# Two weight pieces moved behind the second group's output, and VectorE's order in the first slots

## The chip, the cores and the metric

The kernel runs on one core of one Trainium2 chip. The metric is device microseconds of one execution. A core has five engines with an instruction stream of their own: TensorE (PE in the profile, its weight loads PEld), VectorE (DVE), ScalarE (ACT), GpSimd (POOL) and SyncE (SP), which issues nearly all DMAs here. Each engine runs its instructions in the order in which the program wrote them and waits on semaphores for the others.

## The reference, cut to what matters

Sparse attention of 4 batches, 8 heads, 576 positions and head size 64 (half of the heads look at the last 32 positions, the other half at every fourth of the last 128) gives a matrix of 2304 tokens by 512. Two feed-forward layers of width 2048 follow, each `(act(x @ w_in)) @ w_out`:

```
scores = scale * q @ k.T; scores = where(mask, scores, -1e9)
attn = exp(scores - max(scores)); attn = attn / (sum(attn) + 1e-9); x = attn @ v
h = x @ moe_w_in;  g = maximum(h, 0) + alpha * minimum(h, 0);  x = g @ moe_w_out
h = x @ moe2_w_in; g = where(h >= 1, h, where(h <= -1, 0, (h + 1)**2 / 4)); y = g @ moe2_w_out
```

## The kernel before, in words

All is float32 in accuracy. TensorE gets there by three products of two halves: a matrix is split into a high half (a ScalarE cast, L327) and a low half (the rest, a subtraction on GpSimd or VectorE, L328), and a product is low x high + high x low + high x high (L513 to L515 for the first layer's input side, L706 to L708 for its output side).

Attention is cut into 24 groups of three blocks, six for each batch. The first six groups (batch 0) run at the very start, in the loop `for i in range(NGB)`; the others are spread over the feed-forward slots that follow. Group i of the first six goes through: scores on TensorE (`e_scores`), maximum and subtraction on VectorE and the exponential on ScalarE (`e_exp`, L190, L191, L193), transposes (`a_turn`, L212, copied by ScalarE in L214), values (`e_values`, 48 small matmuls in L205) with the division on VectorE (`a_norm`, L229 to L231), and transposes back (`a_out`, L238) with a ScalarE copy to X (L256). The loop is a pipeline written out by hand: turn i holds the scores of group i, the transposes of i - 1, the exponential of i, the output of i - 2 and the values of i - 1, in this order on every engine.

Weights come in 512 KB pieces, 128 x 1024 words of 32 bits, of which `w_load` (L272) loads one into a staging buffer (five of them at the start). VectorE makes a piece's 128 x 512 float32 from it in three operations that `w_make` returns: L321, L322 and L315. `conv(k)` runs the next k of these operations of the list of pieces. The first two write their intermediate into the weight's own buffer in SBUF as long as `w0_tile` holds nothing, and into a PSUM bank after that. When a piece of the input weights is done, the next `w_cut()` splits it into halves (ScalarE L327, GpSimd L328); the pieces at the start are (rows 0, 1, 2 of w_in), w_out 0, w_in 3, and so on.

In the loop the pieces 0 and 1 are loaded among the six groups' own inputs (the set `FIRST` in L757) and converted at the end of turns 0 and 2 (L817). At the end of turn 3 the first 512 tokens' chunk 0 is split (`x_split`, low half on GpSimd), GpSimd clears a buffer (L821), and SyncE then loads group 6 and more pieces; turn 4 splits chunk 1. Behind the loop come the first layer's rows 0 and 1, one chunk of the input after the other (`f_h(n0, 0, (0,))`, `f_h(n0, 1, (0,))`, ...), with the last two groups' remaining steps between them, three more `conv` calls, and one small VectorE operation that turns alpha into 1 - alpha (L847). Then come the slots: one feed-forward row each, with the activation (ScalarE L650, VectorE L653), the conversions (`EARLY`: five in the first slot) and one point at which attention moves on.

Of the kernel before, what the change touches and what calls it, by code (L numbers as in the profile page):

```python
# [10 lines left out]
F32 = mybir.dt.float32  # L11
# [5 lines left out]
ALU = mybir.AluOpType  # L17
# [3 lines left out]
DM, DFF = 512, 2048  # L21
NT = B * S
P = 128
# [31 lines left out]
NX = 9  # L55
NR = 4

FIRST = (0, 2)

EARLY = (5, 6)  # L60
READY = 12
# [26 lines left out]
def attention_then_two_ffns(ctx: ExitStack, tc: tile.TileContext, a0, aqk, av, w1i, w1o, w2i, w2o, alpha, masks, ident, out, out_l):  # L88
    nc = tc.nc
# [10 lines left out]
    ps_a = ctx.enter_context(tc.tile_pool(name="ps_a", bufs=1, space=bass.MemoryType.PSUM))  # L100
# [3 lines left out]
    al = const.tile([P, NF], F32, name="al")  # L104
# [9 lines left out]
    sc_t, s_t, pT_t, o_t = {}, {}, {}, {}  # L114
# [81 lines left out]
    def e_values(i):  # L196
        pT = pT_t.pop(i)
        ps = ps_e.tile([P, 2, TW], F32, tag="o2", name="o_ps")
        v = e_in[i][:, QK:].rearrange("p (n j d) -> p n j d", n=GS, j=4)
        for n in range(GS):  # L200
            for j in range(4):
                r = slice(j * SUB, (j + 1) * SUB)
                for h in range(2):
                    p = slice(h * D, (h + 1) * D)
                    nc.tensor.matmul(ps[r, h, n * DS:(n + 1) * DS], pT[p, n, r], v[p, n, j], start=True, stop=True)  # L205
        a_norm(i, ps[:, :, :GS * DS].rearrange("p h (n d) -> p n h d", n=GS))
# [19 lines left out]
    def a_norm(i, ps):  # L226
        o = tmp(i).tile([P, GS, 2, D], F32, tag="o", name="o")
        rs = st_p.tile([P, GS, 2, 1], F32, tag="rs", name="rs")
        nc.vector.tensor_scalar(rs, ps[:, :, :, D:], 1e-9, None, ALU.add)  # L229
        nc.vector.reciprocal(rs, rs)  # L230
        nc.vector.tensor_tensor(o, ps[:, :, :, :D], rs.to_broadcast([P, GS, 2, D]), ALU.mult)  # L231
        o_t[i] = o
# [32 lines left out]

    st_free = [f"v{i}" for i in range(NX - NST, NX)]

    def w_load(ph, f, part):
        w = ((w1i, w1o), (w2i, w2o))[ph][part]
        tag = st_free.pop(0)  # L270
        st = xv_p.tile([P, DM, 2], I32, tag=tag, name="st") if tag in xv_tags else pools[tag].tile([P, DM, 2], I32, tag=tag, name="st")
        nc.sync.dma_start(st.rearrange("p a b -> p (a b)"), w[f].bitcast(I32))  # L272
        cv[ph, f, part] = (st, tag)

# [2 lines left out]
    w0_tile = [None]  # L277
# [48 lines left out]
    def two(hi, lo, src, low_on):  # L326
        nc.scalar.activation(hi, src, AF.Copy)  # L327
        low_on.tensor_tensor(lo, src, hi.bitcast(F32), ALU.subtract)  # L328
# [29 lines left out]
    def w_split(n, f):  # L358
        t = r_slot((n, f))
        two(t[:, 0], t[:, 1], wi[n[0], f], nc.vector if n == PAIRS[0] and f < 2 else nc.gpsimd)  # L360
        wt[n, f] = t
        b = base.get((n[0], f // 2))
        if b:
            b[1] -= 1
            if not b[1]:
                x_free.append(b[0])

    def w_cut():
        while cut:
            w_split(*cut.pop(0))  # L370
# [46 lines left out]
    def x_slot(n):  # L417
        tag = x_free.pop(0)
        x_tags.setdefault(n, []).append(tag)
        return pools[tag].tile([P, 2, TW], F32R, tag=tag, name="xv")  # L420

    def x_split(n, c, on_pool=False):
        ph, t = n
        t0, w = TILES[ph][t]
        at = 0
        if w < TW and c % 2:
            x, at = xt[n, c - 1][0], w
        else:
            x = x_slot(n)
        two(x[:, 0, at:at + w], x[:, 1, at:at + w], X[c][:, t0:t0 + w], nc.gpsimd if on_pool else nc.vector)  # L430
        xt[n, c] = (x, at)
# [298 lines left out]
    with tc.manual_schedule(), ExitStack() as late:  # L730
# [19 lines left out]
        pend_l = pieces(0)  # L750
        pend_w = list(pend_l)

        for i in range(NGB):
            a_load_qk(i)
            a_load_v(i)
            if i in FIRST:
                w_load(*pend_l.pop(0))  # L757
            if i == 1:
                nc.sync.dma_start(mask[:, 2 * GS:], masks[:, 2 * GS:])
        nc.sync.dma_start(al, alpha)  # L760
# [26 lines left out]
        def conv(k):  # L787

            for _ in range(k):
                if not todo and pend_w and pend_w[0] in cv:  # L790
                    todo.extend(w_make(*pend_w.pop(0)))
                if todo:
                    todo.pop(0)()
                    if not todo:
                        more()
# [8 lines left out]
        for i in range(NGB):  # L804
            e_scores(i)
            if i >= 1:
                a_turn(i - 1, ps_a, "a")
            e_exp(i)
            if i >= 2:
                a_out(i - 2, ps_a, "w")  # L810
            else:
                fill(2)
            if i >= 1:
                e_values(i - 1)
            w_cut()
            if i in FIRST:
                conv(3)  # L817
            if i == 3:
                x_split(n0, 0, True)

                nc.gpsimd.memset(qk[0], 0.0)  # L821
                hold = False
                a_load_qk(NGB)
                w_load(*pend_l.pop(0))
                w_load(*pend_l.pop(0))
                a_load_v(NGB)
                more()
            if i == 4:
                x_split(n0, 1, True)
        w_cut()  # L830
        f_h(n0, 0, (0,))
        f_h(n0, 1, (0,))
# [10 lines left out]
        f_h(n0, 1, (2,))  # L843
        x_split(n0, 3)
        w_cut()
        conv(1)
        nc.vector.tensor_scalar(al, al, -1.0, 1.0, ALU.mult, ALU.add)  # L847
        a_load_qk(NGB + 1)
        a_load_v(NGB + 1)
        f_h(n0, 0, (3,))  # L850
        f_h(n0, 1, (3,))
        first.close()
        w0_tile[0] = lambda: ps_a.tile([P, DM], F32, tag="w", name="w_ps")
        pools_q = [f"{g}{i}" for g in ("qk", "vz") for i in range(2)]
        pools.update({g: wq for g in pools_q})
        wl_p = late.enter_context(tc.tile_pool(name="wl_p", bufs=1))
# [53 lines left out]
        def one_y():  # L910
            f_y(*pend_y.pop(0))
# [4 lines left out]
        def slot(n, f, k):  # L916
            nn = after_n[n]
            if k not in (1, 2):
                split_pending()
            if k > 1 and (n, f) not in wt:  # L920
                w_cut()
            if n == LAST and f == NF - 1:
                wo_split((n, 0), f)
            if k > 1 or n == LAST:
                f_h(n, f)
            early = f < 2 and k > 1
            if early:
                one_y()
            if n == PLAIN[0] and f == NF - 3:
                pend_l.extend(pend_2)  # L930
            if n == PLAIN[0] and f == NF - 1:
                pend_w.extend(pend_2)
            if n in PLAIN[:2] and f >= NF - NC:
                x_split(nn, f - NF + NC, n == PLAIN[1])
            if k in (0, 1):
                ops = EARLY[k]
            elif n == n0:
                ops = 6
            elif n != LAST:
                ops = 1 if n == PLAIN[1] else 3  # L940
            else:
                ops = 0
            attention_point()
            if k == 2:
                split_pending()
            b0, b1 = BEFORE[n[0]]
            b0 = min(ops, b0) if k else 0
            g = f_g(n, f, lambda: conv(b0))
            ops -= b0
            first_ops = min(ops, b1 if k else 3)  # L950
            w_cut()
            conv(first_ops)
            f_cut(n, f, g)
            if k == 0:
                wo_split((n, 0), f)
            ahead = 2 if n == PLAIN[0] else 3
            for i in range(1, ahead + 1):
                if f + i < NF:
                    ready(n, f + i)
                elif nn and nn not in PAIRS:  # L960
                    ready(nn, f + i - NF)
            if n == PLAIN[2]:
                if f == 9:
                    turn = iter(range(1 << 30))
                    x_work.extend(x_seven(nn, lambda: ps_a.tile([P, TW], F32, tag="w" if nxt < NG or at else "wa"[next(turn) % 2], name="room")))
                if NF - 4 <= f < NF - 1:
                    p_weights(nn, 0, f - NF + 4)
                if READY <= f < NF - 1:
                    wo_split((n, 0), f)
                if f >= READY:  # L970
                    more_x((6, 6, 3, len(x_work))[f - READY])
                if f == NF - 1:
                    p_weights(nn, 0, 3)
                if f == NF - 1:
                    r_free.extend(x_free[:2])
                    del x_free[:2]
            if n == LAST and f % 2 == 0 and 4 <= f // 2 + 3 < NF // 2:
                w_base(1, f // 2 + 3)
            if k >= 2 and not early:
                one_y()  # L980
            pend_y.append(((n, 0), f))
            attention_point()
            if n == PLAIN[2] and f in (9, 10):
                more_x(3)
            conv(ops - first_ops)
            more()

        k = 0
# [235 lines left out]
```

## Time and profile before

| | |
|---|---|
| median of 3 runs | 848.47 us (847.82 to 849.39) |
| the profiled execution's own time | 848.41 us |
| its span, first to last instruction | 846.3 us |
| TensorE busy, matmuls | 831.4 us, 98% |
| VectorE busy | 514.4 us, 61% |
| ScalarE busy | 459.3 us, 54% |
| GpSimd busy | 483.1 us, 57% |
| mean granted TensorE clock | 0.996 of 2.4 GHz |

Times in the profile's rows are microseconds from the span's start; a mean of one instruction is in ns. A busy time is the union of an engine's instructions. The profiled execution took 2.1 us more than its span, for what lies before the first and behind the last instruction.

### The profile page before, as it was taken

Reading aid. Unit: us, or ns where it says so; the run is one execution under the profiler, and the core shown is the slowest. Engines: PE = TensorE matmul, PEld = TensorE weight load, DVE = VectorE, ACT = ScalarE, POOL = GpSimd, SP = SyncE. Lnnn points to the kernel's source line nnn. Section 1 sums busy time; section 2 is a strip of 40 time slices with the busy share of each in tenths; the row PEclk is TensorE's granted clock in tenths of the full one; section 3 lists DMA queues with packets and bytes.
Section 4 is the critical chain, followed back from the end, with each engine's and each line's share of the span. In section 5 each row is a group of like instructions: output and inputs, shape, how many; then the busy total and the mean of one; then the engine's idle time right before and its main releaser. Section 6 shows DMA issues by size and latency. Waiting matters only on the chain.

```text
span 846.3 us, 14045 instructions
## 1 busy us (share of the span) xinstructions
PE 831.4 (98%) x5232; PEld 681.3 (81%) x5234; DVE 514.4 (61%) x831; ACT 459.3 (54%) x883; POOL 483.1 (57%) x411
## 2 busy tenths in 40 slices
PE   6999999999999999999999999999999999999998
PEld 3667778998777878888888888888888888888897
DVE  4798787666775676776688565665326556530132
ACT  3444444665435465555444677675437666553375
POOL 2465656777434677767448676754662332346485
PEclk9899999999999999999999999999999999999999
DMA  8788665864640025444287735343835553538120
GB/s 303 240 252 228 203 171 179 257 196 135 191 129 26 1 75 180 144 154 169 100 312 301 282 142 204 127 173 121 327 125 203 196 198 125 174 134 313 69 82 25
DMA packets 54978, 147.43 MB, mean 174 GB/s; under 512 B 5632, under 2 KB 13440, under 8 KB 54912
## 3 DMA queue, kind: packets, MB, share of 16 engines
q1 hardware_dynamic: 54624, 146.39, 50.9%
q8 instruction: 41, 0.67, 0.3%
q14 instruction: 25, 0.20, 0.1%
q10 hardware_dynamic: 288, 0.16, 0.1%
HBM read 101.97 MB, written 44.56 MB: 173 GB/s over the span
## 4 chain that ended last, share of the span: by engine, by line
PE 92%; DVE 4%; ACT 1%; issue 1%; DMA 1%; ACTq 0%; DVEq 0%
PE y L706 14%; PE y L707 14%; PE y L708 14%; PE h_ps L544 9%; PE h_ps L546 9%; PE h_ps L545 9%; PE h_ps L513 5%; PE h_ps L515 5%; PE h_ps L514 5%; PE o_ps L223 2%; PE s_ps L149 1%; PE t_ps L212 1%; PE y L691 1%; PE y L692 1%; PE y L693 1%
## 5 line engine op out<-in xcount | busy, mean ns | idle before, releaser
L328 POOL TENSOR_TENSOR wol<-wo,woh 128x512 fp32r<-128x512 f32 x153 | 201.8, 1326 | 74.5 <-ACT woh L327 64.4
L328 POOL TENSOR_TENSOR wr<-wb,wr 128x512 fp32r<-128x512 f32 x60 | 77.8, 1297 | 130.3 <-ACT wr L327 130.3
L706 PE MATMUL y<-gh,wol 128*128 128x512 f32 (+1 forms) x384 | 146.3, 381 | 0.0
L708 PE MATMUL y<-gl,woh 128*128 128x512 f32 (+1 forms) x384 | 142.8, 372 | 0.0
L707 PE MATMUL y<-gh,woh 128*128 128x512 f32 (+1 forms) x384 | 142.8, 372 | 0.0
L328 POOL TENSOR_TENSOR wr<-wi,wr 128x512 fp32r<-128x512 f32 x50 | 64.6, 1293 | 121.2 <-ACT wr L327 119.9
L544 PE MATMUL h_ps<-xv,wr 128*128 128x512 f32 x336 | 131.3, 391 | 0.5 <-DVE gl L666 0.4
L546 PE MATMUL h_ps<-xv,wr 128*128 128x512 f32 x336 | 130.8, 389 | 0.0
L545 PE MATMUL h_ps<-xv,wr 128*128 128x512 f32 x336 | 130.8, 389 | 0.0
L327 ACT ACTIVATE woh<-wo 128x512 fp32r<-128x512 f32 x153 | 93.5, 626 | 65.7 <-PE y L708 51.3
L513 PE MATMUL h_ps<-xv,wr 128*128 128x512 f32 (+1 forms) x256 | 89.9, 351 | 0.2
L514 PE MATMUL h_ps<-xv,wr 128*128 128x512 f32 (+1 forms) x256 | 86.3, 337 | 0.2 <-DVE xv L328 0.2
L515 PE MATMUL h_ps<-xv,wr 128*128 128x512 f32 (+1 forms) x256 | 86.4, 337 | 0.0
L706 PEld LDWEIGHTS y<-gh,wol 128*128 128x128 f32 x384 | 72.2, 188 | 15.2 <-issue 2.0
L708 PEld LDWEIGHTS y<-gl,woh 128*128 128x128 f32 x384 | 72.2, 188 | 13.0 <-DVE gl L581 0.4
L707 PEld LDWEIGHTS y<-gh,woh 128*128 128x128 f32 x384 | 72.3, 188 | 11.8
L544 PEld LDWEIGHTS h_ps<-xv,wr 128*128 128x128 f32 x336 | 63.1, 188 | 15.8 <-issue 1.4
L706 PE MATMUL y<-gx,wol 128*128 128x512 f32 x192 | 74.8, 390 | 0.0
L707 PE MATMUL y<-gx,woh 128*128 128x512 f32 x192 | 74.7, 389 | 0.0
L708 PE MATMUL y<-gx,woh 128*128 128x512 f32 x192 | 74.7, 389 | 0.0
L566 DVE SCALAR_TENSOR_TENSOR h_ps<-h_ps,g 128x512 f32<-128x512 f32 x64 | 44.6, 697 | 48.3 <-ACT g L558 48.3
L546 PEld LDWEIGHTS h_ps<-xv,wr 128*128 128x128 f32 x336 | 63.1, 188 | 13.2
(130 smaller groups left out, 1552.3 us busy)
## 6 DMA issues: line engine op xcount, KB each, us to landing
gd<-XA SPq DMA_DIRECT2D x42, 512.0 KB, 3.3
gx<-gd SPq DMA_DIRECT2D x42, 512.0 KB, 6.5
wb<-whole SPq DMA_DIRECT2D x30, 512.0 KB, 5.1
st<-w1i SPq DMA_DIRECT2D x16, 512.0 KB, 5.2
st<-w1o SPq DMA_DIRECT2D x16, 512.0 KB, 5.3
st<-w2i SPq DMA_DIRECT2D x16, 512.0 KB, 4.2
st<-w2o SPq DMA_DIRECT2D x16, 512.0 KB, 4.9
kept<-wr SPq DMA_DIRECT2D x16, 512.0 KB, 2.7
```

The lines of the kernel that those rows point to most:

```text
L327: nc.scalar.activation(hi, src, AF.Copy)
L328: low_on.tensor_tensor(lo, src, hi.bitcast(F32), ALU.subtract)
L513: nc.tensor.matmul(ps[:, :w], r[:, 1, cs], x[:, 0, xs], start=(c == 0), stop=False)
L514: nc.tensor.matmul(ps[:, :w], r[:, 0, cs], x[:, 1, xs], start=False, stop=False)
L515: nc.tensor.matmul(ps[:, :w], r[:, 0, cs], x[:, 0, xs], start=False, stop=(c == NC - 1))
L544: nc.tensor.matmul(o, w[:, 1, cs], x[:, 0], start=start and m == 0, stop=False, skip_group_check=not start)
L545: nc.tensor.matmul(o, w[:, 0, cs], x[:, 1], start=False, stop=False, skip_group_check=not start)
L546: nc.tensor.matmul(o, w[:, 0, cs], x[:, 0], start=False, stop=m == 1, skip_group_check=not start)
L566: ve.scalar_tensor_tensor(ps, ps, 1.0, t, ALU.max, ALU.min)
L706: nc.tensor.matmul(o, wl[:, cs], gh[:, :w], start=(i == 0), stop=False)
L707: nc.tensor.matmul(o, wh[:, cs], gh[:, :w], start=False, stop=False)
L708: nc.tensor.matmul(o, wh[:, cs], gl[:, :w], start=False, stop=(i == NF - 1))
```

## The change

`FIRST` becomes (3, 4): the first two pieces are converted at the end of turns 3 and 4. They are no longer loaded among the groups' inputs; in turn 2, behind the second group's `a_norm`, VectorE copies one element of that group's output into each staging buffer, and the two loads wait for those copies. The 1 - alpha operation moves to the end of turn 4. The PSUM intermediate of the conversions begins one `conv` earlier, with the fourth piece. In the first slot two conversions instead of three run ahead of the point at which attention moves on, and three instead of two behind it.

```
-FIRST = (0, 2)
+FIRST = (3, 4)
...
-    def w_load(ph, f, part):
+    def w_load(ph, f, part, behind=None):
...
+        if behind is not None:
+            nc.vector.tensor_copy(st[:, 0, :1].bitcast(F32), behind[:, 0, 0, :1])
         nc.sync.dma_start(st.rearrange("p a b -> p (a b)"), w[f].bitcast(I32))
...
             a_load_v(i)
-            if i in FIRST:
-                w_load(*pend_l.pop(0))
...
                 e_values(i - 1)
+            if i == 2:
+                for _ in FIRST:
+                    w_load(*pend_l.pop(0), o_t[1])
             w_cut()
             if i in FIRST:
                 conv(3)
...
             if i == 4:
                 x_split(n0, 1, True)
+                nc.vector.tensor_scalar(al, al, -1.0, 1.0, ALU.mult, ALU.add)
...
         w_cut()
+        w0_tile[0] = lambda: ps_a.tile([P, DM], F32, tag="w", name="w_ps")
         conv(1)
-        nc.vector.tensor_scalar(al, al, -1.0, 1.0, ALU.mult, ALU.add)
...
         first.close()
-        w0_tile[0] = lambda: ps_a.tile([P, DM], F32, tag="w", name="w_ps")
...
-            first_ops = min(ops, b1 if k else 3)
+            first_ops = min(ops, b1 if k else 2)
```

## Rows read from the trace of the kernel before

**Rows 1.** The page: busy us, share, instructions; the instruction queue's packets, MB, share.
```profile
PE 831.4 (98%) x5232; PEld 681.3 (81%) x5234; DVE 514.4 (61%) x831; ACT 459.3 (54%) x883; POOL 483.1 (57%) x411
...
q8 instruction: 41, 0.67, 0.3%
```
**Rows 2.** Stretches: length, busy by PE, PEld, DVE, ACT, POOL; clock, DMA, GB/s.
```profile
36.30:44.70 8.40, 7.84 (x58) 5.51 (x56) 8.11 (x14) 3.99 (x8) 3.30 (x3) 1.00 1.06 281
44.70:56.00 11.30, 9.95 (x88) 7.51 (x88) 10.92 (x20) 4.64 (x10) 7.60 (x6) 1.00 0.93 291
56.00:80.00 24.00, 23.86 (x195) 18.13 (x194) 20.11 (x35) 11.25 (x22) 15.30 (x12) 1.00 0.74 210
```
**Rows 3.** TensorE's instructions in order: start, length, line, operands, count, idle before and releaser.
```profile
14.47 0.72 PE L205 MATMUL o_ps<-e_in,pT 64*32 64x65 f32 x48 [1.63 <-ACT s L193]
...
17.23 0.42 PE L205 MATMUL o_ps<-e_in,pT 64*32 64x65 f32 x23 [0.32 <-ACT pT L214]
20.74 0.66 PE L205 MATMUL o_ps<-e_in,pT 64*32 64x65 f32 x25 [3.08 <-issue]
...
24.14 0.98 PE L205 MATMUL o_ps<-e_in,pT 64*32 64x65 f32 x48
...
29.11 0.39 PE L513 MATMUL h_ps<-xv,wr 128*128 128x512 f32 x1
```
**Rows 4.** DMA in 17.66:18.2, 18.2:18.3; GB/s by 40 slices in 17.66:20.74, 20.74:24.
```profile
q1 hardware_dynamic: 105, 0.18, 92.7%
...
q8 instruction: 1, 0.02, 69.1%
...
GB/s 327 365 489 250 408 290 185 330 62 43 41 43 50 0 41 0 41 41 0 41 0 81 41 0 41 41 41 3 4 0 3 4 0 0 0 0 0 0 0 0
...
GB/s 0 0 0 0 0 0 0 0 0 0 0 0 201 0 0 0 0 0 0 0 0 0 0 0 0 0 0 0 0 0 0 0 0 0 0 0 0 0 0 0
```
**Rows 5.** Stretches of 2 us, columns as in rows 2 (the clock is third from the end).
```profile
12.00:14.00 2.00, 0.84 (x8) 0.70 (x7) 1.11 (x2) 1.22 (x4) 1.27 (x1) 1.00 1.02 391
...
20.00:22.00 2.00, 1.26 (x47) 0.79 (x55) 0.47 (x3) 1.31 (x4) 1.12 (x1) 0.50 0.03 8
...
26.00:28.00 2.00, 1.75 (x74) 1.34 (x57) 1.26 (x3) 0.75 (x2) 1.28 (x1) 0.82 0.84 226
```
**Rows 6.** DMA issues at 0.74 and 1.66 us: KB, us from issue to landing.
```profile
e_in<-a SPq DMA_DIRECT2D x1, 416.0 KB, 3.7
...
st<-w1i SPq DMA_DIRECT2D x1, 512.0 KB, 5.3
```
**Rows 7.** VectorE's instructions in order.
```profile
15.22 0.17 DVE L229 TENSOR_SCALAR rs<-o_ps 128x6 f32<-128x6 f32 x1 [1.93 <-PE o_ps L205]
...
16.12 0.42 DVE L321 TENSOR_SCALAR wi<-st 128x512 int32<-128x512 int32 x1
...
17.91 0.55 DVE L190 TENSOR_REDUCE mx<-s_ps 128x6 f32<-128x384 f32 x1
...
35.37 1.52 DVE L321 TENSOR_SCALAR wo<-st 128x512 int32<-128x512 int32 x1
36.81 0.16 DVE L847 TENSOR_SCALAR al<-al 128x16 f32<-128x16 f32 x1
37.09 0.75 DVE L653 SCALAR_TENSOR_TENSOR g<-g,al,h_ps 128x512 f32<-128x512 f32 x1
```
**Rows 8.** ScalarE's instructions in order.
```profile
19.15 0.52 ACT L193 ACTIVATE s<-s 128x384 f32<-128x384 f32 x1 [1.97 <-DVE s L191]
...
36.28 0.60 ACT L650 ACTIVATE g<-h_ps 128x512 f32<-128x512 f32 x1 [1.03 <-PE h_ps L515]
```
**Rows 9.** GpSimd's instructions in order.
```profile
20.88 1.27 POOL L328 TENSOR_TENSOR wr<-wi,wr 128x512 fp32r<-128x512 f32 x1 [7.42 <-ACT wr L327]
...
23.32 1.17 POOL L821 MEMSET qk<- 128x1280 f32 x1
```
**Rows 10.** VectorE by line in 36.3:56: count, busy us, mean ns, idle before.
```profile
L321 DVE TENSOR_SCALAR w_ps<-st 128x512 int32<-128x512 int32 x6 | 4.2, 692 | 0.1
```

More of the change, by code (lines that the diff above doesn't have):

```diff
@@ L56 @@
 NR = 4
-FIRST = (0, 2)
+FIRST = (3, 4)
 EARLY = (5, 6)
@@ L266, in attention_then_two_ffns, with w_load @@
     st_free = [f"v{i}" for i in range(NX - NST, NX)]
-    def w_load(ph, f, part):
+    def w_load(ph, f, part, behind=None):
         w = ((w1i, w1o), (w2i, w2o))[ph][part]
@@ L271, in w_load @@
         st = xv_p.tile([P, DM, 2], I32, tag=tag, name="st") if tag in xv_tags else pools[tag].tile([P, DM, 2], I32, tag=tag, name="st")
+        if behind is not None:
+            nc.vector.tensor_copy(st[:, 0, :1].bitcast(F32), behind[:, 0, 0, :1])
         nc.sync.dma_start(st.rearrange("p a b -> p (a b)"), w[f].bitcast(I32))
@@ L755, in attention_then_two_ffns @@
             a_load_v(i)
-            if i in FIRST:
-                w_load(*pend_l.pop(0))
             if i == 1:
@@ L814, in attention_then_two_ffns @@
                 e_values(i - 1)
+            if i == 2:
+                for _ in FIRST:
+                    w_load(*pend_l.pop(0), o_t[1])
             w_cut()
@@ L829, in attention_then_two_ffns @@
                 x_split(n0, 1, True)
+                nc.vector.tensor_scalar(al, al, -1.0, 1.0, ALU.mult, ALU.add)
         w_cut()
@@ L845, in attention_then_two_ffns @@
         w_cut()
+        w0_tile[0] = lambda: ps_a.tile([P, DM], F32, tag="w", name="w_ps")
         conv(1)
-        nc.vector.tensor_scalar(al, al, -1.0, 1.0, ALU.mult, ALU.add)
         a_load_qk(NGB + 1)
@@ L852, in attention_then_two_ffns @@
         first.close()
-        w0_tile[0] = lambda: ps_a.tile([P, DM], F32, tag="w", name="w_ps")
         pools_q = [f"{g}{i}" for g in ("qk", "vz") for i in range(2)]
@@ L949, in slot @@
             ops -= b0
-            first_ops = min(ops, b1 if k else 3)
+            first_ops = min(ops, b1 if k else 2)
             w_cut()
```

## The prediction

> **What bounds the kernel now.** I read the page's busy shares first. TensorE is busy 831.4 of 846.3 us and no other engine passes 61% [rows 1], so only a stretch in which TensorE is not full can change the time. The stretches come next: from 56 to 80 us TensorE is busy 23.86 of 24 us, and from 36.3 to 56 it lacks 1.9 us while VectorE is busy 19.0 of 19.7 [rows 2]; before that it waits for whatever ends a short chain. Both edits lie before 43 us. After that each microsecond by which the start ends earlier or later reaches the end one for one, so the whole question is when the start ends.
>
> The instruction order of that start is the third view. TensorE stands still twice: 1.63 us up to 14.47 and 3.08 us up to 20.74, the second in the middle of 48 like matmuls (23 before it, 25 after) [rows 3]. The page's instruction queue has 41 packets of 16 KB (0.67 MB / 41); TensorE has 10,466 instructions, 255 for each packet [rows 1]. Between the two stops lie 127 matmuls with as many weight loads (48 + 50 + 3 + 3 + 23), 254. So both are stops for instructions. The packet that ends the second one is not among the transfers up to 18.2 us and is there at 18.2 to 18.3, when the queue of loads runs dry [rows 4]; TensorE goes on about 2.5 us later. After that stop the granted clock is 0.5, which is the 1.2 GHz level; it is 2.4 GHz after the shorter stop and again from 26.7 us (0.82 of 26 to 28 at two levels) [rows 5].
>
> By the Trainium skill (Runtime: NRT & Kernel Launch, section Instruction fetch mechanics) instructions come in 16 KiB blocks by a DMA queue of the engine, and the cost of a block's end is mostly hidden. The packet size agrees with the trace; hidden it is not here, with 3.08 us.
>
> **Part 1, the two weight pieces.** Removed from the front of the load queue: 2 x 512 KB of about 6 MB. The queue moves about 0.4 MB per us there [rows 5], so it runs dry 2.6 us earlier, at 15.6 instead of 18.2. The second stop shrinks, but not by all of that: a block's end is crossed at 14.47, and the packet for the block after that cannot come at once: behind the crossing at 20.74, with no load queued, it came in the 13th of 40 slices of 20.74 to 24, about 1.0 us later [rows 4]. Before, some of the 16 engines had loads until 19.8 (the bytes in the 40 slices of 17.66 to 20.74 end in the 28th), so until 17.2 now. With the packet at 15.6 to 17.2 TensorE goes on at 18.1 to 19.7; bounds 17.66 (no stop) and 20.74 (as before). I take 19.4, nearer the late end, because the packet has to pass the loads of its own engine.
>
> What is late next? Three things move onto VectorE behind it. Each conversion of a piece is L321, L322, L315: 16.12 to 17.91, 1.79 us; the three operations of a group's output are 0.90 (15.22 to 16.12); maximum and subtraction are 1.24 (17.91 to 19.15) [rows 7, 8]. Before, the pieces were converted right behind the scores of group 0 and the output of group 1, and TensorE's stops hid the delay. Now they stand in groups 3 and 4, where scores, maximum, subtraction, output and conversion are one chain. Step by step:
> - Group 1's output ends at 16.12 as before. Two copies of one element: nearest are the 0.17 for 6 elements and nothing; 0.3 for both with their gaps. SyncE then issues the two loads at 16.4; nothing is queued behind them but the loads of group 6, which wait for a GpSimd memset until about 22.
> - The pieces land: a first load of 416 KB on an empty queue took 3.7 us, one of 512 KB behind others 5.3 [rows 6]. So the first lands at 20.1 to 21.7; I take 20.4, as the queue is almost empty, and the second 1.3 us (512 KB) later.
> - Group 2's output starts on VectorE at 20.0 (19.4, the last 25 matmuls 0.5, a gap) and ends at 20.9. Conversion 1.79, maximum and subtraction 1.24, group 3's output 0.90, conversion 1.79, the 1 - alpha operation 0.18 (0.16 [rows 7] and a gap), maximum and subtraction 1.24. Sum 7.14: group 5's subtraction ends at 28.0.
> - Then the second piece is one cast away from TensorE. ScalarE first does group 5's exponential and group 3's output copy, then the high half, and GpSimd the low half: before, from exponential to GpSimd's end, 19.15 to 22.15, 3.0 us [rows 8, 9]. That chain was done at 22.15 and hidden; now it ends at 31.0, and TensorE's first matmul of feed-forward row 1, which ran at 29.11, waits for it [rows 3]. In TensorE's queue behind it stand group 5's transposes, its values, and all that follows to the first slot. Cost: 1.9 us.
> - One collision on top. L321 takes 0.42 us when GpSimd is idle; at 35.37 it took 1.52, with a GpSimd cast of the same time beside it [rows 7]. The first piece's L321 now falls at 20.9, beside the cast of the first token chunk (1.27) and the memset of 128x1280 (1.17), which move forward to 19.7 to 22.1 [rows 9]. Bounds 0 and 1.1 for it. The nearest row is the one at 35.37, so I take 1.1. The second piece's L321 comes ahead of GpSimd's next cast; 0. Part 1 is +3.0 us.
>
> By the Trainium skill (SBUF — State Buffer, Who interferes with whom) the pair of ports that VectorE and GpSimd share is an exclusive lock, and a VectorE operation with two SBUF inputs also stands still for a GpSimd operation that reads SBUF. The 1.52 us agree with the first half. By the second half L322 or L315 of the second piece, whose intermediate still lies in SBUF, would wait for a cast of 1.27 too; no row of before shows it, and the sum would be 1.3 us higher.
>
> **Part 2, VectorE's order.** The fourth piece's L321 at 35.37 writes to PSUM now: 0.69, as the six later ones that do so, instead of 1.52, and the alpha operation is gone from the place. That frees 1.0 us of VectorE, but the operation after them (37.09) needs ScalarE's result, which was ready at 36.88 (36.28 + 0.60) [rows 7, 8, 10]. So only 0.14 us comes forward (37.09 to 36.95); the rest becomes a wait. Taking the maximum ahead of one conversion lets TensorE transpose group 6 sooner, but VectorE has the same work to do up to 56 us and bounds that stretch [rows 2], so I cost it at nothing. Part 2 is -0.14 us, between 0 and -1.0.
>
> **Sum.** +3.0 - 0.14 = +2.9 on the profiled execution's 848.41 us: 851.3. The median shown is 848.47, 0.06 higher, which is nothing here.
>
> **The rivals.**
> - *A wash.* No collision, and the instruction packet comes at 15.6: then TensorE goes on at 18.1, the landing at 20.1 to 20.4 sets the first conversion instead of group 2's output, and the same sum costs 1.1 to 1.4 us; with 0.14 to 1.0 from part 2 that is +0.1 to +1.3: 849.2. For it: the memset may simply wait for VectorE. Against: it needs both.
> - *The clock falls again.* In my forecast TensorE stands from 29.7 (row 0's matmuls done) to 32.1, and 2 us before that for group 5's scores. A stop of 1.63 us left the clock at 2.4 GHz, one of 3.08 did not [rows 3, 5]; mine lie between. At half clock 48 small matmuls took 0.98 against 0.72 [rows 3], a third more; a matmul of 512 columns should lose more, up to double. The clock came back 6 us after the work did. On some 5.4 of the 6.3 us from 29.11 to 35.37 (the rest is other engines' work) that is 1.8 to 3.9; with 2.9, 854.2.
> - *The second stop stays*, because something else than the loads makes it: TensorE goes on at 20.74, 1.3 us later than I say: 852.6. Against it: the packet came as the queue of loads ran dry [rows 4]. The rule of the Trainium skill above (Runtime: NRT & Kernel Launch, Instruction fetch mechanics), with a fetch that is hidden, would make this the case.
> - *Not slower.* Both stops go, as loads of weights no longer stand between those of groups 1 and 3. TensorE then starts group 1's values at 13.1, the pieces are issued at 15.1 and land at 18.8 (3.7 later), and the chain from there (7.14 with 3.0 behind it) ends at 28.9, 0.2 before 29.11; if the freed 1.0 us of part 2 also counts in full, 847.2. The place that decides is the landing of the first piece: each microsecond before 18.8 is one more. Against: the queue of loads moves 0.39 MB per us at the first stop [rows 5] and will be as full there as it was.
>
> **How the numbers follow.** Forecast 0.38 (850.2 to 852.6), clock 0.21, stop stays 0.05, wash 0.21, not slower 0.15, of which 0.09 lies beyond 0.2%. 0.2% is 1.7 us, about what a measurement of this kernel can tell from nothing. So slower 0.64, the same 0.27 (0.21 + 0.06), faster 0.09. The range leaves out the far end of the clock case and most of the gains: 847.4 to 855.5; the slower cases alone span 850.2 to 855.5.
>
> **What would show it.** Right: the second stop about 1.3 us long; the two pieces issued at 16.4 and landed by 20.4 and 21.7; L321 of the first piece over 1 us; TensorE waiting at L513 of row 1 for GpSimd's cast, at 31 to 32; L321 of the fourth piece at 0.69 with a wait for ScalarE behind it. Wrong: row 1's first matmul before 29.1, or the operation of 37.09 earlier than 36.9 in the profile after. The clock line tells the third case apart. If the time from 56 us on is not the same in both profiles, the premise of the first paragraph falls.

## The result, and the profile after

| | before | changed |
|---|---|---|
| median | 848.50 us (4 runs, 847.82 to 849.39) | 855.19 us (4 runs, 854.47 to 856.57) |
| ratio | | 1.0078, 95% interval 1.0064 to 1.0092 |
| the profiled execution's time, span | 848.41, 846.3 | 855.31, 853.3 |

Slower by 0.78%, inside the range and on its far side: 3.9 us more than the 851.3 forecast. The change adds two lines above the ones it shifts, so L321, L322, L315 of before are L323, L324, L317 here, L513 is L515, L653 is L655 and L328 is L330.

TensorE's instructions in the changed kernel (columns as in [rows 3], whose rows these answer to):
```profile
14.84 0.72 PE L205 MATMUL o_ps<-e_in,pT 64*32 64x65 f32 x48 [1.93 <-ACT XA L256]
...
17.61 0.43 PE L205 MATMUL o_ps<-e_in,pT 64*32 64x65 f32 x23 [0.32 <-ACT pT L214]
18.37 0.43 PE L205 MATMUL o_ps<-e_in,pT 64*32 64x65 f32 x25 [0.33 <-issue]
...
23.04 0.30 PE L205 MATMUL o_ps<-e_in,pT 64*32 64x65 f32 x3 [1.55 <-issue]
25.11 0.50 PE L173 MATMUL s_ps<-mask,idt 128*128 128x192 bf16 x2 [1.77 <-DVE s L191]
...
33.82 0.74 PE L515 MATMUL h_ps<-xv,wr 128*128 128x512 f32 x1 [3.34 <-POOL wr L330]
```
The second stop is 0.33 us instead of 3.08, so at 18.37 TensorE is 2.4 us ahead of before. At 25.11 it is level, and at row 1's first matmul it is 4.7 us behind, waiting for GpSimd's cast of the second piece. That is the forecast's place, and 1.7 us later than its 32.1. What stands between is VectorE's chain, to be read against [rows 7]:
```profile
15.60 0.16 DVE L229 TENSOR_SCALAR rs<-o_ps 128x6 f32<-128x6 f32 x1 [2.23 <-PE o_ps L205]
...
16.62 0.21 DVE L273 COPY st<-o 128x1 f32<-128x1 f32 x2
...
20.41 2.06 DVE L323 TENSOR_SCALAR wi<-st 128x512 int32<-128x512 int32 x1 [0.53 <-DMA st<-w1i]
...
25.86 0.42 DVE L323 TENSOR_SCALAR wi<-st 128x512 int32<-128x512 int32 x1
...
27.04 1.65 DVE L317 SCALAR_TENSOR_TENSOR wi<-st,wi 128x512 int32<-128x512 int32 x1
28.61 1.24 DVE L833 TENSOR_SCALAR al<-al 128x16 f32<-128x16 f32 x1
...
30.41 0.56 DVE L191 TENSOR_TENSOR s<-s_ps,mx 128x384 f32<-128x384 f32 x1
```
Three operations are far over what they take alone: 2.06 (0.42 alone), 1.65 (0.69) and 1.24 (0.16). GpSimd in the same time ([rows 9]):
```profile
19.81 1.28 POOL L330 TENSOR_TENSOR xv<-XA,xv 128x512 fp32r<-128x512 f32 x1 [14.97 <-ACT xv L329]
21.02 1.17 POOL L824 MEMSET qk<- 128x1280 f32 x1
26.86 1.28 POOL L330 TENSOR_TENSOR wr<-wi,wr 128x512 fp32r<-128x512 f32 x1 [4.67 <-ACT wr L329]
28.10 1.72 POOL L330 TENSOR_TENSOR xv<-XA,xv 128x512 fp32r<-128x512 f32 x1
32.50 1.26 POOL L330 TENSOR_TENSOR wr<-wi,wr 128x512 fp32r<-128x512 f32 x1 [2.69 <-ACT wr L329]
```
L323 runs from 20.41 to 22.47: through the rest of the cast (to 21.09) and the whole memset (to 22.19), and then the 0.3 us it needs. L317 ends 0.55 us behind the cast of 26.86, the 1 - alpha operation just behind the cast of 28.10, which itself took 1.72 instead of 1.28, with L317 ahead of it (in e5_clear below, where L317 takes 0.69, the same cast takes 1.29).

Stretches of the changed kernel (columns as in [rows 5]):
```profile
24.00:30.00 6.00, 4.89 (x107) 3.56 (x107) 5.76 (x10) 2.70 (x5) 2.96 (x2) 0.50 0.97 291
30.00:34.00 4.00, 0.66 (x3) 0.18 (x2) 2.02 (x6) 1.42 (x3) 1.26 (x1) 0.93 1.04 336
34.00:38.00 4.00, 4.00 (x59) 3.11 (x60) 0.34 (x2) 1.57 (x4) 0.00 (x0) 0.58 0.21 80
```
VectorE is the full engine from 24 to 30; TensorE does 0.66 us of work from 30 to 34; the clock is at 1.2 GHz twice, in 24 to 30 and again in most of 34 to 38, behind the stops of 1.55 and 1.77 and the stop of 3.34 us.

Part 2's place, to be read against the last lines of [rows 7] (the fourth piece's L323, then the first slot's activation):
```profile
41.28 0.69 DVE L323 TENSOR_SCALAR w_ps<-st 128x512 int32<-128x512 int32 x1
42.83 0.75 DVE L655 SCALAR_TENSOR_TENSOR g<-g,al,h_ps 128x512 f32<-128x512 f32 x1 [0.86 <-ACT g L652]
```
0.69 us, and a wait of 0.86 us for ScalarE behind it, as forecast. Here the kernel is 5.74 us behind before (42.83 to 37.09).

### The profile page after: what moved, and what is told of

Its sections match the earlier page's. It is cut to its first block, busy times and chain, and to the rows that moved or that the text cites. A ratio compares the mean times of both kernels' runs of the same rounds, so it can differ in the third digit from the quotient of the medians.

```text
span 853.3 us, 14052 instructions
## 1 busy us (share of the span) xinstructions
PE 833.8 (98%) x5234; PEld 682.3 (80%) x5234; DVE 517.2 (61%) x833; ACT 460.1 (54%) x883; POOL 483.2 (57%) x411
## 4 chain that ended last, share of the span: by engine, by line
PE 84%; DVE 7%; DMA 3%; ACT 3%; POOL 1%; issue 1%; SPq 0%; ACTq 0%; DVEq 0%; POOLq 0%
PE y L708 13%; PE y L710 13%; PE y L709 13%; PE h_ps L546 7%; PE h_ps L548 7%; PE h_ps L547 7%; PE h_ps L515 5%; PE h_ps L516 5%; PE h_ps L517 5%; DMA gd<-XA 2%; PE o_ps L223 2%; PE s_ps L149 1%; PE y L693 1%; PE y L694 1%; PE y L695 1%
## 5 line engine op out<-in xcount | busy, mean ns | idle before, releaser
L330 POOL TENSOR_TENSOR wol<-wo,woh 128x512 fp32r<-128x512 f32 x153 | 201.8, 1326 | 74.6 <-ACT woh L329 64.5
L330 POOL TENSOR_TENSOR wr<-wb,wr 128x512 fp32r<-128x512 f32 x60 | 77.7, 1295 | 130.2 <-ACT wr L329 129.6
L330 POOL TENSOR_TENSOR wr<-wi,wr 128x512 fp32r<-128x512 f32 x50 | 64.6, 1293 | 113.8 <-ACT wr L329 112.5
L515 PE MATMUL h_ps<-xv,wr 128*128 128x512 f32 (+1 forms) x256 | 90.6, 354 | 3.5 <-POOL wr L330 3.3
```

The costliest lines, as they stand in the source:

```text
L515: nc.tensor.matmul(ps[:, :w], r[:, 1, cs], x[:, 0, xs], start=(c == 0), stop=False)
```

## The experiments

My theory going in: the second piece's cast ends late, because two conversions now stand in VectorE's chain, and three VectorE operations stand still for GpSimd on top; the clock adds some. The rivals: it is part 2 that costs; or the moved transfers cost, by delaying instruction packets. Each ratio is against runs of the kernel before on the same chip.

**e1_part1**: part 1 alone.
```
-                nc.vector.tensor_scalar(al, al, -1.0, 1.0, ALU.mult, ALU.add)   # turn 4
+        nc.vector.tensor_scalar(al, al, -1.0, 1.0, ALU.mult, ALU.add)           # old place
...   (PSUM intermediate from the fifth piece, 3 conversions ahead, as before)
```


> The loads and conversions moved, VectorE's order as before. Theory (the second piece's cast ends late, and three VectorE operations stand still for GpSimd): the 1 - alpha operation no longer stands still 1.24 us behind GpSimd's cast, so the first matmul of row 1 comes at 32.4 to 32.8 instead of 33.82 and the time is 853.5 to 854.3. Rival (VectorE's order is what costs): within 1 us of the kernel before, 848.5. A time equal to that of the changed kernel (855.2) would say that the 1 - alpha operation's stand is hidden.


Measured: 852.71 us, ratio 1.0051 (1.0034 to 1.0068). Row 1's first matmul:
```profile
32.78 0.79 PE L515 MATMUL h_ps<-xv,wr 128*128 128x512 f32 x1 [3.00 <-POOL wr L330]
```
32.78, 1.04 us sooner than in the changed kernel, as expected. The time is 0.8 below what I expected; the profiled execution, at 855.16, was the longest of four (the others 852.4 to 852.8), so how much of the 2.5 us between the two medians is this one operation stays open. In that execution the 1.04 us were lost again: the granted clock is 0.50 from 34 to 38 us (0.58 in the changed kernel), and the transposes behind the next row come at 38.96, against 38.95 there. Part 1 alone is above before by its whole interval, so it is what costs most.

**e2_part2**: part 2 alone (`FIRST = (0, 2)`, loads among the groups' inputs).

> VectorE's order changed, loads and conversions as before. Theory: nothing to speak of, 847.8 to 848.8; the fourth piece's first conversion takes 0.69 us and a wait of 0.8 us follows it; the 1 - alpha operation may stand still for the cast beside it at 26 us and shift the next maximum by under 1 us, hidden. Rival (VectorE's order costs): above 851.


Measured: 848.66 us, ratio 0.9997 (0.9986 to 1.0009), the same. VectorE at the fourth piece:
```profile
34.75 0.69 DVE L323 TENSOR_SCALAR w_ps<-st 128x512 int32<-128x512 int32 x1
36.29 0.75 DVE L655 SCALAR_TENSOR_TENSOR g<-g,al,h_ps 128x512 f32<-128x512 f32 x1 [0.85 <-ACT g L652]
```
The 0.83 us that L323 no longer takes are a wait of 0.85. Part 2 costs nothing by itself. In part 1's company it does: there the 1 - alpha operation lies in a chain with no slack, here (1.00 us long at 25.70) row 1's first matmul does not wait for it.

**e3_psum**: the changed kernel with the PSUM intermediate from the first piece on.
```
+        w0_tile[0] = lambda: ps_a.tile([P, DM], F32, tag="w", name="w_ps")   # ahead of the loop
         for i in range(NGB):
```


> The changed kernel with the PSUM intermediate from the first piece on. Theory: the first piece's first operation takes 0.69 instead of 2.06 us and the second piece's last one 0.69 instead of 1.65, so row 1's first matmul comes 2.1 to 2.6 us sooner (31.2 to 31.7), TensorE's stop before it shrinks under 1.5 us, its clock does not fall a second time (another 1.0 us): 851.5 to 852.8. Rival (the loads behind the output delay the instruction packets, and that costs): within 0.7 of the changed kernel, 855.2.


Measured: 854.29 us, ratio 1.0072 (1.0057 to 1.0087): a miss. Row 1 did come at 31.77, but TensorE's transposes of the group outputs use the same bank, and wait for the conversion now (the second line is VectorE's):
```profile
22.65 0.88 PE L238 MATMUL x_ps<-idt,o 128*128 128x128 f32 x3 [2.68 <-DVE wi L317]
...
24.47 0.17 DVE L229 TENSOR_SCALAR rs<-o_ps 128x6 f32<-128x6 f32 x1 [0.91 <-PE o_ps L205]
...
27.65 0.87 PE L238 MATMUL x_ps<-idt,o 128*128 128x128 f32 x3 [1.05 <-DVE wi L317]
...
38.97 0.52 PE L238 MATMUL x_ps<-idt,o 128*128 128x128 f32 x3 [1.92 <-DVE wi L317]
```
The first holds up the values behind it, for which VectorE's chain waits 0.91 us; the second is beside the path; the last one took back what row 1 had won. L323 at 20.36 and L317 at 26.82 take 0.70 and 0.69 here, so this run says nothing against the collisions, and a bank of its own was needed.

**e4_fill**: the changed kernel with idle matmuls in TensorE's two longest waits.
```
+            if i == 5:
+                fill(6)
             e_scores(i)
...
         f_h(n0, 0, (0,))
+        fill(8)
         f_h(n0, 1, (0,))
```


> The changed kernel with 6 and 8 idle matmuls of 128x512 before group 5's scores and before row 1's first matmul, which keep TensorE busy in its two longest waits. Theory: the clock stays up behind row 1, 1.0 us of the loss goes: 853.8 to 854.5; the wait itself is as long. If the clock is most of the loss, below 852.5. If the clock does not matter, 855.2 or later.


Measured: 853.92 us, ratio 1.0067 (1.0048 to 1.0085), as expected, though the interval overlaps the changed kernel's. In the profiled execution the clock stays up:
```profile
24.00:30.00 6.00, 4.85 (x114) 2.96 (x114) 5.72 (x10) 2.58 (x5) 2.96 (x2) 1.00 1.03 279
...
34.00:38.00 4.00, 3.75 (x67) 2.98 (x66) 1.94 (x5) 1.55 (x5) 0.00 (x0) 1.00 0.25 94
```
and row 1 comes at 33.36, 0.46 us sooner (the first piece was converted from 19.85, 0.56 sooner). This execution, at 852.06, was the shortest of four. By the times alone the clock's share is not settled; what the rows make of it, about 1 us of the loss and not its cause, is worked out under *The clock* below.

**e5_clear**: the changed kernel without any collision: the first two pieces' intermediate in a PSUM bank that nothing else uses then, 1 - alpha at its old place.
```
+        w0_tile[0] = lambda: ps_h.tile([P, DM], F32, tag="h", name="w_ps")   # ahead of the loop
...
+        w0_tile[0] = None                                                    # behind the loop
```


> The changed kernel with the first two pieces' intermediate in a PSUM bank that nothing else uses then, and the 1 - alpha operation at its old place: no VectorE operation of the chain stands still for GpSimd, and TensorE waits for no bank. Theory: row 1's first matmul at 30.9 to 31.4 (33.82 in the changed kernel, 29.11 before), one fall of the clock at most, 850.3 to 851.8, so what is left is the length of the chain, some 2 us. Rival (the GpSimd collisions are not it): above 853.


Measured: 851.84 us, ratio 1.0047 (1.0029 to 1.0065); 0.04 us above the range I expected. The conversions and row 1:
```profile
20.57 0.70 DVE L323 TENSOR_SCALAR w_ps<-st 128x512 int32<-128x512 int32 x1 [0.24 <-DMA st<-w1i]
...
26.10 0.69 DVE L317 SCALAR_TENSOR_TENSOR wi<-st,w_ps 128x512 int32<-128x512 int32 x1
```
```profile
30.76 0.79 PE L515 MATMUL h_ps<-xv,wr 128*128 128x512 f32 x1 [2.63 <-POOL wr L330]
```
No operation of the chain is long any more, and row 1 comes 3.06 us sooner than in the changed kernel. The other 1.65 us of its 4.71 are the length of the chain (some 0.5 of them because L323 into PSUM takes 0.70 and 0.68 instead of 0.42).

**e6_loads_early**: the changed kernel with its two loads back among the groups' inputs; only the conversions are late.

> The changed kernel with the two loads back among the groups' inputs; only the conversions stay late. Theory: the second stop of TensorE is long again (2 to 3 us instead of 0.33), group 2's output and the chain behind it start some 2 us later, row 1's first matmul at 35 to 36, 856 to 857.5: the moved loads by themselves gain. Rival (the moved loads are what costs, by their transfers beside the instruction packets): 853 or less.


Measured: 855.70 us, ratio 1.0088 (1.0073 to 1.0104), 0.3 us below what I expected. TensorE, then VectorE:
```profile
20.81 0.61 PE L205 MATMUL o_ps<-e_in,pT 64*32 64x65 f32 x25 [3.05 <-issue]
...
34.13 0.80 PE L515 MATMUL h_ps<-xv,wr 128*128 128x512 f32 x1 [4.47 <-POOL wr L330]
```
```profile
22.37 0.42 DVE L323 TENSOR_SCALAR wi<-st 128x512 int32<-128x512 int32 x1
22.82 0.69 DVE L324 SCALAR_TENSOR_TENSOR wi<-st,wi 128x512 int32<-128x512 int32 x1
```
The stop is back at 3.05 us, so it is the two loads in front that make it. But row 1 is only 0.31 us later, where my theory had it at 35 to 36: here L323 finds GpSimd idle and takes 0.42, and L324 begins at 22.82 against 22.50 in the changed kernel. So the 2.4 us that the moved loads won were spent within 4 us: 0.53 on the landing, 1.64 in the collision. The rival that the moved transfers cost falls, and so does my theory that they gain by themselves: the two times differ by less than their intervals.

**e7_cut_early**: e5_clear, with the second piece's split right behind its conversion.
```
             if i in FIRST:
                 conv(3)
+            if i == 4:
+                w_cut()
```


> The collision-free version (first two pieces' intermediate in a free PSUM bank, 1 - alpha late) with the second piece's split moved ahead: right behind its conversion in turn 4, before group 5's exponential and group 3's output copy on ScalarE. Theory (the place of the second piece's cast in the chain is what TensorE waits for): row 1's first matmul at 28.2 to 29.2 instead of 30.76, no stop over 1.2 us before it, no fall of the clock: 847.8 to 849.5, level with the kernel before. Rival (the late scores of group 5 bound it anyway): 850.5 or more.


Measured: 849.56 us (10 runs), ratio 1.0017 (1.0006 to 1.0027); TensorE at group 4's values and at row 1:
```profile
27.58 0.73 PE L205 MATMUL o_ps<-e_in,pT 64*32 64x65 f32 x48 [2.67 <-ACT pT L214]
...
29.06 0.40 PE L515 MATMUL h_ps<-xv,wr 128*128 128x512 f32 x1
```
29.06 is before's 29.11, and moving one split took away the stop in front of row 1. That shows the mechanism: what stood ahead of the split on ScalarE decided when row 1 could start. TensorE still stops, for 2.67 us in front of group 4's values, since ScalarE now copies their transposes behind the split; I had expected no stop over 1.2 us. The time is 0.06 us above what I expected and still a little above before; the profiled execution is at 847.91, so where the other executions lose 1.6 us is not seen.

**v1_one_late** and **v2_group5_late** ask whether the shorter second stop can be had without the late conversions. The first moves only the second piece (`FIRST = (0, 3)`, PSUM as in e5_clear); the second leaves the pieces where they were and puts group 5's own loads behind the second group's output.

> Only the second piece is late (behind the second group's output, converted in turn 3, intermediate in PSUM); the first is loaded and converted as before; 1 - alpha at its old place. Theory: the second piece's cast is done by 26, off TensorE's path; TensorE's second stop is about 1 us and the clock stays up, group 5's scores come at 23.3 to 24 (25.05 before): 846 to 848. Rival (any late conversion puts its 1.8 us on the path): 849 to 850.5.

> The kernel before with group 5's own two loads (806 KB) behind the second group's output, and the weight pieces where they were. Theory: the loads' queue runs dry 2 us earlier, the second stop shrinks to about 1 us, no conversion moves: group 5's scores at 22 to 23.5 instead of 25.05, 845.5 to 847.5. Rival (group 5's input is then late itself, landing at 20.5 to 22 and waiting for nothing else): within 1 us of before, 848.5. If the stop does not come from the loads: 848.5 as well, with the stop of 3 us still there.


Measured: 848.44 us, ratio 1.0007 (0.9997 to 1.0017), and 849.70 us, ratio 1.0008 (0.9995 to 1.0021). Neither gains; v1 is 0.44 us above what its theory allowed, v2 2.2. In v1:
```profile
19.48 0.43 PE L205 MATMUL o_ps<-e_in,pT 64*32 64x65 f32 x25 [1.43 <-issue]
...
24.23 0.34 PE L173 MATMUL s_ps<-mask,idt 128*128 128x192 bf16 x2 [0.47 <-DVE s L191]
```
and in v2, TensorE and VectorE:
```profile
18.52 0.43 PE L205 MATMUL o_ps<-e_in,pT 64*32 64x65 f32 x25 [0.82 <-issue]
...
31.63 0.52 PE L238 MATMUL x_ps<-idt,o 128*128 128x128 f32 x3 [1.20 <-DVE o L231]
```
```profile
30.16 0.43 DVE L321 TENSOR_SCALAR wi<-st 128x512 int32<-128x512 int32 x1 [3.52 <-DMA st<-w1i]
```
The stop shrinks to 1.43 and 0.82 us, about as thought. In v2's profile TensorE is 2.75 us ahead at row 1's first matmul (26.36), and then VectorE stands 3.52 us for the third piece, whose load waits in SyncE's queue behind group 6's, which wait for GpSimd's memset. Both profiled executions, at 847.48 and 847.14, were the shortest of ten, so what the others lose is not seen.

**v3_piece_first**: v2 with that piece's load issued ahead of group 6's.

> The kernel with group 5's loads late, and the third weight piece's load issued ahead of group 6's, so that it does not wait for GpSimd's memset. There VectorE had stood 3.5 us for that piece and TensorE 1.2 us behind it. Theory: the stop of 1.2 us goes and the start ends 2.2 us sooner than before, 845.8 to 847.2. Rival (the piece's transfer then delays an instruction packet, or the gain is lost to the next wait): within 0.2% of before, 847.5 to 849.5.


Measured: 847.45 us (11 runs), ratio 0.9994 (0.9985 to 1.0002): the same as before. TensorE:
```profile
24.29 0.30 PE L205 MATMUL o_ps<-e_in,pT 64*32 64x65 f32 x3 [1.31 <-issue]
```
The time lies between the two ranges; the trace has the rival's mechanism: a stop for instructions at the next block's end, whose packet comes at 21 to 22 us among the piece's transfer (issued at 17.65, landed 5.2 us later), gives back 1.31 us. None of these versions is measurably faster than before.

## Why the prediction was right or wrong, point by point

Direction, place and range held; the likeliest value was 3.9 us low. That the time lies inside the range is in part luck: its upper end came from a fall of the clock, priced at 2.9 us, which cost 1.2, and collisions that were not in the sum filled the gap. By its own steps:

- *The premise* (what the start loses reaches the end) held nearly: ScalarE's activation of the first slot is 5.91 us behind (42.19 against 36.28), and from 42 to 320 us of before the lag of its operations stays between 5.8 and 6.0. Around 325 to 365 us another 0.7 came, at stores of 512 KB for which ScalarE waits (before, then changed):
```profile
355.59 0.60 ACT L576 ACTIVATE XA<-h_ps 128x512 fp32r<-128x512 f32 x1 [1.82 <-DMA gd<-XA]
362.25 0.60 ACT L578 ACTIVATE XA<-h_ps 128x512 fp32r<-128x512 f32 x1 [2.49 <-DMA gd<-XA]
```
  The store took 6.6 us to land, 6.0 before. e1_part1's and e6_loads_early's profiles gain as much at these stores, e5_clear's does not, e4_fill's loses 0.6; why stays open.
- *The second stop* was forecast to end at 19.4, which leaves 1.7 us of it; the 1.3 named among the signs is what it would lose. It was 0.33. I had let the packet wait for its engine's last loads. It made little difference: the first piece landed at 20.4, as forecast, and took over as the bound, so the conversion began at 20.41 instead of 20.9.
- *The chain* was forecast at +1.9 us on row 1's matmul; e5_clear, which has only that, shows +1.65, and e7_cut_early shows that it is this chain.
- *The collisions* are the step that failed: one, at 1.1 us, where there were three, with 3.06 us together on row 1 (33.82 to 30.76). The first I had sized from a single GpSimd operation; the waiting VectorE operation was passed over by a second one, and took 1.64 us more instead of 1.1. The 1 - alpha operation I entered at 0.18 us and it took 1.24. And L317, which I put at nothing in the sum, took 0.96 more. Together that is 2.6 us over the sum; with the conversion 0.5 sooner and the steps between 0.4 shorter it gives the 1.7 us by which row 1 missed 32.1.
- *The rule that I weighed and left out of the sum* was right. By the Trainium skill (SBUF — State Buffer, Who interferes with whom) an operation with two SBUF inputs stands still for a GpSimd operation that reads SBUF. L317 beside the cast shows it here: 1.65 us with its intermediate in SBUF, 0.69 in PSUM in e5_clear. The 1.3 us that the prediction named for it were 0.96.
- *The clock* was a rival and came true, for 1.2 us and not 2.9. Row 0's next matmul, before and changed:
```profile
31.54 0.50 PE L513 MATMUL h_ps<-xv,wr 128*128 128x512 f32 x1
37.46 0.50 PE L515 MATMUL h_ps<-xv,wr 128*128 128x512 f32 x1
```
  The lag has grown from 4.71 us at row 1's first matmul to 5.92. In e5_clear, where the clock falls there too, it grows from 1.65 to 2.75; in e4_fill, where it stays up, only from 4.25 to 4.34. The clock is back at about 37.3 (granted clock 0.50 from 34 to 37 us, 0.68 from 37 to 37.5, 1.00 behind that), 3.5 us after the work, where I had taken the 6 us of before. The range of my price has an error as well: a third of 5.4 us is the 1.8, but double would add 5.4 and not 3.9. And the two stops that I set my own between, 1.63 and 3.08 us, do not bound anything: the last section has a fall behind 1.67.
- *Part 2* was forecast at -0.14 and nothing for the new order; by itself it is -0.03% with an interval of 0.1% either way. What I missed is its part in the collisions.

So 1.65 (chain) + 3.06 (collisions) + 1.2 (clock) + 0.7 (stores) = 6.6, of 6.9 between the profiled executions. This adds up two single executions; from median to median the loss is 6.7.

## What to carry to other kernels

When work moves on an in-order engine, price it beside its new neighbours: a duration from a row in which the other engine was idle is a lower end. Here GpSimd's casts and its memset were the neighbours that counted. A stop that is removed is worth only the distance to what comes next on that path (here the landing of the moved load, 2 us on). When a piece of work becomes late, look for what is queued between its end and its user on every engine: moving the split ahead of the next turn's other ScalarE operations brought row 1 back to its old place.

## What the runs showed of the hardware that was not expected

- A VectorE operation that stood still for GpSimd was not let in between two GpSimd operations back to back: L323 took 2.06 us through a cast and a memset (2.06 in e1_part1, 2.17 in e4_fill), where it takes 0.42 with GpSimd idle (e6_loads_early).
- A VectorE operation of 128 x 16 elements took 1.24 us beside a GpSimd cast, 0.16 without one.
- TensorE's stops for instructions move with the load queue: 3.08 us with the two pieces in front (3.05 when they were put back; in e2_part2, with them in front too, TensorE came to it later, stood 2.12 us and went on at 20.76, as at 20.74 in before), 0.33 without them. But then 1.55 us at the next block's end, 252 TensorE instructions on: that block's packet came at 20.6 to 20.8, while the moved pieces kept the DMA engines busy (97% of 18.3 to 21.0). Taking bytes out of one stretch put the stop into another.
- The clock fell in one execution where the same instructions kept it in another. Up to 20 us TensorE's instructions in the kernel before and in e2_part2 are the same, and so, nearly, is the first stop (1.63 and 1.67 us); behind it (columns as in [rows 5], before, then e2_part2) the clock is at 2.4 GHz in one and at 1.2 GHz in the other:
```profile
16.00:18.00 2.00, 1.34 (x40) 0.90 (x29) 1.93 (x5) 0.49 (x1) 0.00 (x0) 1.00 1.04 400
16.00:18.00 2.00, 2.00 (x42) 1.43 (x25) 1.93 (x5) 0.49 (x1) 0.00 (x0) 0.50 1.03 400
```
